# Chunked attention and a gated feed-forward: the second product of the last two blocks in seven products, and another order at the beginning

## The chip, the cores and the metric

One Trainium2 chip, one core. The metric is the device time of one execution in microseconds (us), the median of the runs shown; lower is better. Five engines work side by side: TensorE (PE), VectorE (DVE), ScalarE (ACT), GpSimd (POOL), and SyncE (SP), which issues nearly all DMAs from one queue, in order.

## The reference

q, k and v are 8 x 8 heads x 576 positions x 64, in float32. Attention is within chunks of 64 positions: scores of a chunk are scaled by 1/8, go through a softmax, and weigh v of the same chunk. The result is laid out as x, 4608 tokens x 512. Then

```
h = x @ w_in                              # 512 x 2048, float64 weights
g = h * (1.0 / (1.0 + np.exp(-1.702 * h)))
out = (g @ w_out).astype(np.float32)      # 2048 x 512
```

## The kernel before, in words

**Precision.** Each float32 operand of the feed-forward is split into a high part in TensorE's float32r format and a low part (the rest), and a product is three matmuls: high x high, high x low, low x high, summed in PSUM. The weights arrive as 8-byte words and are converted on the chip by `plan_w`, one column block j of 128 of the 2048 at a time (1 MB of w_in and w_out together): ACT scales (`scale`, L287, `low`, L291), DVE shifts and joins (`shift`, L296, `join`, L300), ACT takes the high part (L305), DVE the low part (L310).

**Blocks.** Tokens go in 36 tiles of 128; four tiles are a block of 512, nine blocks in all. In the first three blocks ("plain", `plan_ffn`) each j has a first product (`h_pe`, L1134 to L1136, 12 matmuls of 512 columns; for the first two j in two halves of 256 columns, `h_half`, L1145 to L1147), the gating on ACT (L1155), its split by ACT and DVE (`g_hi`, L1156, and `g_lo`, L1161), and a second product (`o_pe`, L1171 to L1173, per tile 3 matmuls of 512 columns that add up in the tile's PSUM bank over 16 j).

**Seven products.** The last six blocks go in three pairs (s = 0, 1, 2). Their first product is made by `plan_two` in the scheme of Strassen and Winograd: operands are cut into 2 x 2 quarters, and 7 products of quarters replace 8. A pair has 8 steps p of two column blocks each, every step 7 products (L701 to L703, 6 matmuls of 512 columns), drained by ACT and DVE (`drain`, L714 and L686). The combinations of w_in are made once by `plan_prep` on POOL, ACT and DVE, written to the DRAM tensor `seven`, and read back in pieces of 256 KB into six buffers. The combinations of x (`plan_x`) stay in the slots of w_in that are then free. The second product of these blocks is the plain one: 16 j x 4 tiles x 3 matmuls of 512 columns for each block, from g split by `high` (L744) and `low` (L748).

**Attention.** Tiles 0 to 3 go one by one (`plan_first`): q, k and v rows come by `load_rows` (L359), one DMA for a tile's q and one for its k, 256 KB in packets of 256 bytes (64 floats of one head and position); PE transposes them (L398), ACT and DVE copy them, scores (L419), softmax on DVE, ACT and POOL, transposes of the weights (L447), and x (L463). Later tiles go in pairs (`plan_pair`), whose transposes are made by DVE from the third pair on (L898 and L963).

**Order.** Nothing is ordered by hand in the code: every step is given to `Plan` with its engine, a cost, a rank, the events that it needs, and the buffers that it takes and gives. `Plan.emit` plays the steps through, at each moment starting on each free engine the ready step of least rank, and writes the instructions in that order. Three things overrule the ranks: `ORDER`, which lists the first steps of every engine, `NUDGE`, which adds to the rank of some 70 steps, and `FILL`, three groups of unused matmuls of the identity (`keep_warm`, L1244) among the first steps of PE. One rank unit is one j of a plain block.

## Time and profile before

| | us |
|---|---|
| median of three runs | 829.34 (827.34 to 829.91) |
| span of the profiled execution, first to last instruction | 826.6 |
| PE busy in the span | 814.7 |
| DVE busy | 526.5 |
| ACT busy | 371.2 |
| POOL busy | 94.7 |

Of the profiled execution only its span is given; the three runs are timed without a profile, the lowest of them 0.7 us above that span. Busy time is the union of an engine's instructions. A PE matmul is recorded for longer than the distance to the next one, so PE's rate is read from the starts of neighbouring matmuls.

### The profile page before, as it was taken

How to read it: one execution, taken by the hardware profiler on the slowest of the kernel's cores; microseconds unless marked ns; L12 is line 12 of the kernel's file. 1: busy time of each engine (PE TensorE's matmuls, PEld its weight loads, DVE VectorE, ACT ScalarE, POOL GpSimd, SP SyncE). 2: the span in 40 equal slices, each digit the busy share in tenths (PEclk: the TensorE clock that was granted, in tenths of full speed). 3: DMA queues.
4: the chain of work that ended last, by engine and by line, in shares of the span. 5: the costliest groups of instructions: out<-in, count | busy, mean ns of one | idle time of the engine just before them, and what ended most of it. 6: DMA issues, size and time to landing. Idle time of an engine off the chain costs nothing.

```text
span 826.6 us, 14741 instructions
## 1 busy us (share of the span) xinstructions
PE 814.7 (99%) x5750; PEld 674.1 (82%) x5750; DVE 526.5 (64%) x717; ACT 371.2 (45%) x545; POOL 94.7 (11%) x82
## 2 busy tenths in 40 slices
PE   8899999999999999999999999999999999999998
PEld 7788787888888888888888788888888888888886
DVE  5778977366477789673588686843978543443422
ACT  5889824234346545433446253422653332223322
POOL 1001070000065660000000000000001000000000
PEclk9999999999999999999999999999999999999999
DMA  9998755342386567755574337664441054444101
GB/s 241 323 284 253 235 149 122 56 89 39 68 231 184 121 163 206 189 140 141 145 175 130 50 73 194 169 166 128 128 130 38 26 153 127 119 114 125 52 1 51
DMA packets 233637, 114.24 MB, mean 138 GB/s; under 512 B 185952, under 2 KB 208480, under 8 KB 233568
## 3 DMA queue, kind: packets, MB, share of 16 engines
q1 hardware_dynamic: 233568, 113.30, 52.7%
q8 instruction: 45, 0.74, 0.4%
q14 instruction: 24, 0.20, 0.1%
HBM read 89.13 MB, written 24.12 MB: 137 GB/s over the span
## 4 chain that ended last, share of the span: by engine, by line
PE 87%; DVE 4%; SPq 2%; DMA 2%; ACT 2%; issue 1%; DVEq 0%; ACTq 0%
PE po L1171 15%; PE po L1173 14%; PE po L1172 14%; PE hp L703 9%; PE hp L702 9%; PE hp L701 9%; PE hp L1134 4%; PE hp L1136 4%; PE hp L1135 4%; PE s L914 2%; PE x L988 2%; SPq L359 1%; DMA first_b<-in_v_dram 1%; SPq L855 1%; DMA seven<-w 1%
## 5 line engine op out<-in xcount | busy, mean ns | idle before, releaser
L1171 PE MATMUL po<-w,g_l 128*128 128x512 f32 x576 | 226.5, 393 | 1.1 <-DVE g_l L1161 0.7
L1173 PE MATMUL po<-w,g_h 128*128 128x512 f32 x576 | 224.3, 389 | 0.0
L1172 PE MATMUL po<-w,g_h 128*128 128x512 f32 x576 | 224.3, 389 | 0.0
L1171 PEld LDWEIGHTS po<-w,g_l 128*128 128x128 f32 x576 | 108.1, 188 | 24.6 <-DVE g_l L1161 0.8
L1173 PEld LDWEIGHTS po<-w,g_h 128*128 128x128 f32 x576 | 108.1, 188 | 22.7
L1172 PEld LDWEIGHTS po<-w,g_h 128*128 128x128 f32 x576 | 108.2, 188 | 21.8
L739 ACT ACTIVATE g<-g 128x512 f32<-128x512 f32 x48 | 30.3, 632 | 133.6 <-DVE g L686 133.6
L963 DVE STREAM_TRANSPOSE eT<-e 32x512 f32<-32x512 f32 x120 | 84.2, 702 | 5.1 <-POOL e L944 3.3
L701 PE MATMUL hp<-w,w 128*128 128x512 f32 x224 | 87.1, 389 | 0.0
L702 PE MATMUL hp<-w,w 128*128 128x512 f32 x224 | 87.1, 389 | 0.0
L703 PE MATMUL hp<-w,w 128*128 128x512 f32 x224 | 87.1, 389 | 0.0
L944 POOL TENSOR_TENSOR e<-e,r 128x1024 f32<-128x1024 f32 x16 | 31.6, 1973 | 457.5 <-DVE r L941 255.3
L1134 PE MATMUL hp<-x_l,w 128*128 128x512 f32 x184 | 72.2, 392 | 0.7 <-DVE g_l L1161 0.5
L1136 PE MATMUL hp<-x_h,w 128*128 128x512 f32 x184 | 71.8, 390 | 0.4 <-DVE w L310 0.4
L1135 PE MATMUL hp<-x_h,w 128*128 128x512 f32 x184 | 71.6, 389 | 0.0
L748 DVE TENSOR_TENSOR g_l<-g,g_h 128x512 fp32r<-128x512 f32 x48 | 34.8, 724 | 48.6 <-ACT g_h L744 48.5
L744 ACT ACTIVATE g_h<-g 128x512 fp32r<-128x512 f32 x48 | 30.3, 631 | 75.6 <-PE po L1173 75.3
L898 DVE STREAM_TRANSPOSE qkT<-raw 128x1024 f32<-128x1024 f32 x30 | 37.2, 1242 | 32.9 <-DMA raw<-in_k_dram 19.1
L1161 DVE TENSOR_TENSOR g_l<-hp,g_h 128x512 fp32r<-128x512 f32 (+1 forms) x50 | 33.1, 662 | 35.8 <-ACT g_h L1156 35.4
L686 DVE TENSOR_TENSOR d<-hp,d 128x512 f32<-128x512 f32 x48 | 33.0, 687 | 31.0 <-PE hp L703 30.8
L1155 ACT ACTIVATE hp<-hp 128x512 f32<-128x512 f32 (+1 forms) x50 | 28.4, 569 | 47.8 <-PE hp L1136 43.4
L702 PEld LDWEIGHTS hp<-w,w 128*128 128x128 f32 x224 | 42.1, 188 | 8.7
(117 smaller groups left out, 1206.1 us busy)
## 6 DMA issues: line engine op xcount, KB each, us to landing
w<-seven SPq DMA_DIRECT2D x112, 256.0 KB, 2.9
pieces<-seven SPq DMA_DIRECT2D x56, 256.0 KB, 2.8
seven<-w SPq DMA_DIRECT2D x24, 512.0 KB, 3.8
raw<-in_moe_w_in_dram SPq DMA_DIRECT2D x16, 512.0 KB, 7.7
raw<-in_moe_w_out_dram SPq DMA_DIRECT2D x16, 512.0 KB, 7.1
out_dram<-ob SPq DMA_DIRECT2D x31, 256.0 KB, 3.0
raw<-in_q_dram SPq DMA_DIRECT2D x208, 32.0 KB, 2.1
raw<-in_k_dram SPq DMA_DIRECT2D x208, 32.0 KB, 2.1
```

The source lines that it names most:

```text
L701: nc.tensor.matmul(hp, w[:, 0, c], xl[:, c], start=c == 0, stop=False)
L702: nc.tensor.matmul(hp, w[:, 0, c], xh[:, c], start=False, stop=False)
L703: nc.tensor.matmul(hp, w[:, 1, c], xh[:, c], start=False, stop=c == 1)
L748: nc.vector.tensor_tensor(gl, words(h, late), gh.bitcast(F32), op=ALU.subtract)
L898: nc.vector.transpose(st["tr"][:, i].rearrange("p n (t j) -> p (n t) j", j=32), st["raw"][:, i].rearrange("p n t j -> p (n t) j"),)
L963: nc.vector.transpose(st["et"][po : po + 32, :, 32 * a : 32 * a + 32], st["e"][pi : pi + 32, :, 32 * b : 32 * b + 32],)
L1134: nc.tensor.matmul(hp, wh, xl, start=cc == 0, stop=False)
L1135: nc.tensor.matmul(hp, wh, xh, start=False, stop=False)
L1136: nc.tensor.matmul(hp, wl, xh, start=False, stop=cc == NCC - 1)
L1171: nc.tensor.matmul(po, gl[:, c], w[:, 0, :], start=first, stop=False)
L1172: nc.tensor.matmul(po, gh[:, c], w[:, 0, :], start=False, stop=False)
L1173: nc.tensor.matmul(po, gh[:, c], w[:, 1, :], start=False, stop=last)
```

## The change

It has five parts.

1. **The second product of blocks 7 and 8** (pair s = 2) is made by `plan_o` in seven products of quarters: P4, P1, P5, P7, P3, P6, P2, each over the 8 steps p. A step of a product is 4 tiles x 3 matmuls of 256 columns. Its left operand is a quarter of g of one step p (or a sum of quarters, made in place on DVE: S1 to S4), split by ACT and DVE (`hi` and `lo`) into one of 16 pairs of buffers. Sums of PSUM banks and copies at the end of products (`rd_a1`, `rd_c1`, `c45`, `rd_cX`, `C21`, `C12`, `C22`) give three quarters of the output, P2 with `ends` the fourth, one tile after another.
2. **Combinations of w_out** for four of the seven (`plan_four`): for each p, two sums, four differences and four splits, on DVE and ACT, after the transposes of the weights in attention pairs 22 to 32; they use the attention's buffer `e` and the output's `ob`, go to a DRAM tensor `four`, and come back in 32 pieces of 256 KB.
3. **Pair s = 2 of `plan_two`** runs its 56 products without second products between them (`LASTSTEP`), with two more PSUM banks, and leaves all of g in quarters.
4. **Another beginning.** q and k of two tiles come in one DMA each, 512 KB in packets of 512 bytes (two positions); the transposes become 16 matmuls of 64 x 64 with the identity in place of 4 of 128 x 128. For j = 0 and 1 w_in and w_out are loaded and converted apart (`HALVES`).
5. **The order**: `ORDER`, `NUDGE` and `FILL` go; a table `AT` gives some 250 steps a rank of their own. By it the first DMAs are q and k of tiles 0 and 1, w_in of j = 0, q and k of tiles 2 and 3, v of tiles 1 and 2, w_out of j = 0, w_out of j = 1, both of j = 7, w_in of j = 1, v of tiles 3 and 0, then j = 3 and j = 2.

Cut to its core:

```diff
--- before.py
+++ after.py
...
+AT = {
+    "ld0_0_0": -499.23, "q_0": -296.77, "k_0": -295.51, "raw_0_0": -285.26, "tkp_1": -126.62, "m_0": -86.9,
+    "et_0": -82.39, "wsc_2": -82.01, "raw_0_1": -50.23, "pouts0_7": -45.8057, "raw_1_1": -44.052, "raw_7":
+    -39.292, "raw_1_0": -32.312, "v_3": -32.302, "pouts1_7": -29.0457, "v_0": -26.272, "raw_3": -23.042,
+    "raw_2": -18.532, "qk_0_2_8": -7.5, "wshift_2": -5.028, "xh_3": -3.524, "wj_14": -3.15, "wshift_9": -2.126,
+    "h0_10": -1.7, "gl_10": -1.5, "o_8_0": 0.5, "raw_4": 2.954, "qk_0_1_8": 3.5, "qk_0_3_8": 3.98, "raw_11":
+    4.166, "raw_5": 4.704, "pout0_1": 5, "raw_13": 5.01, "P4_0_5": 5.24, "pout0_6": 7.24, "raw_9": 7.436,
+    "o_1_3": 7.73, "mx_4": 7.836, "w_12": 9.76, "m_4": 9.906, "wshift_15": 10.79, "w_7": 10.902, "o_2_0": 14.43,
...
+}
...
-        rank += self.nudge.get(make, 0.0)
+        rank = self.at.get(make, rank)
...
-    FILL = (5, 2, 5)
+    FILL = ()
...
+    LASTSTEP, OSTEP = 1.75, 2.11
+    RING, AHEAD, AHEAD_S = 16, 2.0, 2.2
+    OSTART = START[-1] + LASTSTEP * NF / 2 + 0.1
+    FOUR = (22, 22, 24, 26, 28, 30, 30, 32)
+    LAST = [n for n in range(NB - 2, NB)]
...
+    HALVES = (0, 1)
...
+        parts = ((0, 1), (1, 1)) if j in HALVES else ((0, 2),)
...
+            def load():
+                w_raw[key] = const.tile([P, width], I64, tag=tag, name=f"raw_{name}")
+                if m == 0:
+                    nc.sync.dma_start(
+                        w_raw[key][:, :512].rearrange("p (cc f) -> p cc f", cc=NCC),
+                        w_in[:, j * P : (j + 1) * P].rearrange("(cc p) f -> p cc f", p=P),
+                    )
+                if m + n == 2:
+                    nc.sync.dma_start(w_raw[key][:, width - 512 :], w_out[j * P : (j + 1) * P, :])
...
         def load(i):
+            if ("first", u) not in held:
+                a = const.tile([P, 2048], F32, tag=slot(0), name=f"first_a_{u}")
+                held["first", u] = a.rearrange("p (i h e d) -> p i h e d", i=2, h=H, e=2)
+            for b, s, o, c in spans(u * P, 2 * P):
+                nc.sync.dma_start(
+                    held["first", u][o // 2 : (o + c) // 2, i].rearrange("p h e d -> p h (e d)"),
+                    (q, k)[i][b, :, s : s + c, :].rearrange("h (j e) d -> j h (e d)", e=2),
+                )
...
+            rows = slice(64 * t2, 64 * t2 + 64)
             for n in range(NP):
-                nc.tensor.transpose(
-                    st["ps", i][:, n], st["raw"][:, i, 2 * n : 2 * n + 2, :].rearrange("p h d -> p (h d)"), ident
-                )
+                for e in range(2):
+                    for h in range(2):
+                        nc.tensor.matmul(
+                            st["ps", i][64 * h : 64 * h + 64, n].rearrange("p (t e) -> p t e", e=2)[:, :, e],
+                            held["first", u - t2][rows, i, 2 * n + h, e],
+                            ident[rows, rows],
+                            start=True,
+                            stop=True,
+                        )
...
-        plan.add(DMA, (1, 1.2, 1024), u - 103, lambda: load(0), make=ev("q"), take=[slot(0)])
-        plan.add(DMA, (1, 1.2, 1024), u - 102.9, lambda: load(1), make=ev("k"))
+        if t2 == 0:
+            plan.add(DMA, (1, 1.5, 1024), u - 103, lambda: load(1), make=ev("k"), take=[slot(0), f"w{NF - 3 - 2 * u}"])
+            plan.add(DMA, (1, 1.5, 1024), u - 102.9, lambda: load(0), need=[ev("k")] * 0, make=ev("q"))
+            plan.add(None, 0, u - 95, None, need=[ev("s"), f"s_{u + 1}"], give=[slot(0), f"w{NF - 3 - 2 * u}"])
...
+        def bank(i):
+            q = 7 * p + i
+            return f"po{2 + q // 2 % 2}" if last and q % 2 else "hp"
...
+    T_ORDER = ("T1", "T3", "T4", "T2")
...
+    def plan_four(p):
...
+        def whole(u):
+            if u == 0:
+                st["a"] = const.tile([P, 2, 2, 256], F32, tag="e", name=f"four_a_{p}")
+            w = wt[2 * p + u][:, 1].bitcast(F32)
+            nc.vector.tensor_tensor(
+                st["a"][:, u].rearrange("p k f -> p (k f)"), w[:, 0], w[:, 1], op=ALU.add
+            )
+
+        def sums():
+            (b11, b12), (b21, b22) = [[st["a"][:, u, k] for k in range(2)] for u in range(2)]
+            tt = nc.vector.tensor_tensor
+            tt(b11, b12, b11, op=ALU.subtract)
+            tt(b12, b22, b12, op=ALU.subtract)
+            tt(b22, b22, b11, op=ALU.subtract)
+            tt(b21, b21, b22, op=ALU.subtract)
...
+        u = FOUR[p]
+        rank = RANKS[(u - TB) // 2] - 5
+        e = lambda a: f"{a}_{p}"
+        plan.add(DVE, 0.69, rank, lambda: whole(0), need=[f"et_{u}"] + ([f"tlo3_{p - 1}"] if p else []), make=e("ta0"), take=["e"], port=True)
+        plan.add(DVE, 0.69, rank, lambda: whole(1), need=[e("ta0")], make=e("ta"), port=True)
+        plan.add(DVE, 1.7, rank, sums, need=[e("ta")], make=e("tsum"), port=True)
+        for i in range(4):
+            plan.add(ACT, 0.36, rank, lambda i=i: hi(i), need=[e("tsum")] + [e(f"tlo{i - 1}")] * (i > 0), make=e(f"thi{i}"), take=["ob"])
+            plan.add(
+                DVE, 0.41, rank, lambda i=i: lo(i), port=True, need=[e(f"thi{i}")], make=e(f"tlo{i}"), give=["e"] * (i == 3),
+            )
+            plan.bulk(0.8, rank, lambda i=i: out4(i), need=[e(f"tlo{i}")], make=e(f"tout{i}"), give=["ob"], after=4.0)
+        plan.add(None, 0, rank, None, need=[e(f"tout{i}") for i in range(4)], make=e("tout"))
...
+    def plan_o():
...
+        PRODUCTS = (
+            ("P4", "Y", True, (1, 1), "T4"),
+            ("P1", "X", True, (0, 0), (0, 0)),
+            ("P5", "Z", True, (1, 1), "T1"),
+            ("P7", "Y", False, (0, 1), "T3"),
+            ("P3", "Z", False, (0, 1), (1, 1)),
+            ("P6", "X", False, (1, 1), "T2"),
+            ("P2", "W", True, (1, 0), (1, 0)),
+        )
...
+            open_, stop = fresh and (t % 2 == 0 or a == "W"), p == H - 1
+            nc.tensor.matmul(o, gh[:, c], w[:, 0], start=open_ and p == 0, stop=False, skip_group_check=not open_)
+            nc.tensor.matmul(o, gh[:, c], w[:, 1], start=False, stop=False, skip_group_check=not open_)
+            nc.tensor.matmul(o, gl[:, c], w[:, 0], start=False, stop=stop, skip_group_check=not open_)
...
+        def w_add(what, by, p, fn, need):
+            plan.add(DVE, 0.69, rank(number[by], p) - AHEAD_S, fn, port=True, need=need, make=f"{what}_o_{p}")
+
+        for p in range(H):
+            w_add("S1", "P5", p, lambda p=p: sum_((1, 1), (0, 1), (1, 1), ADD)(p), [f"cl_{number['P4']}_{p}", ge(p, 0, 1)])
+            w_add("S3", "P7", p, lambda p=p: sum_((0, 1), (0, 0), (0, 1), SUB)(p), [f"S1_o_{p}", ge(p, 0, 0)])
+            w_add("S2", "P3", p, lambda p=p: sum_((1, 1), (1, 1), (0, 0), SUB)(p), [f"cl_{number['P5']}_{p}", f"S3_o_{p}"])
+            w_add("S4", "P3", p, lambda p=p: sum_((0, 1), (1, 0), (1, 1), SUB)(p), [f"S2_o_{p}", f"cl_{number['P7']}_{p}", ge(p, 1, 0)])
...
+                take = (["g"] if r < 2 else []) if n < RING else [f"cb{r}"]
+                need = [source[name](p)] + ([freed[r - 2]] if 2 <= n < RING else [])
+                if n:
+                    need.append(f"ch_{(n - 1) // H}_{(n - 1) % H}")
+                plan.add(ACT, 0.6, rank(q, p) - AHEAD, lambda q=q, p=p, r=r: hi(q, p, r), need=need, make=f"ch_{q}_{p}", take=take)
+                plan.add(DVE, 0.69, rank(q, p) - AHEAD, lambda q=q, p=p: lo(q, p), port=True, need=[f"ch_{q}_{p}"], make=f"cl_{q}_{p}")
...
+                plan.add(
+                    PE, 1.44, rank(q, p), lambda q=q, p=p, kk=kk: [mm(q, p, t, kk) for t in range(TB)], need=need + [before],
+                    make=f"O{q}_{p}", take=take, give=give,
+                )
...
+        for t in range(TB):
+            for p in range(H):
+                plan.add(
+                    PE, 0.36, rank(END, 2 * t + p / 4), lambda p=p, t=t: mm(END, p, t, None), need=[f"cl_{END}_{p}", before],
+                    make=f"O{END}_{p}_{t}", take=[BANKS["W"][t]] if p == 0 else [],
+                )
...
+        for i in range(2):
+            both = lambda n, i=i: f"{n}_{i}"
+            plan.add(ACT, 0.6, after("P4"), lambda i=i: copy("Y", i, "a1"), need=[done("P4")], make=both("rd_a1"), take=["tmp"] * (1 - i))
+            plan.add(ACT, 0.6, after("P1"), lambda i=i: copy("X", i, "c1"), need=[done("P1")], make=both("rd_c1"), take=["ob", "ob"] * (1 - i))
+            plan.add(DVE, 0.69, after("P5"), lambda i=i: with_("Z", i, "a1", "a1", SUB), need=[done("P5"), both("rd_a1")], make=both("c45"))
+            plan.add(ACT, 0.6, after("P6"), lambda i=i: copy("X", i, "c12"), need=[done("P6")], make=both("rd_cX"), take=["tmp"] * (1 - i))
+            plan.add(DVE, 0.69, after("P6"), lambda i=i: with_("Y", i, "c21", "c12", ADD), need=[both("rd_cX"), done("P7")], make=both("C21"), take=["tmp"] * (1 - i), give=[BANKS["Y"][i]])
+            plan.add(DVE, 0.69, after("P6"), lambda i=i: with_("Z", i, "c12", "c12", ADD), need=[both("C21"), done("P3")], make=both("C12"))
+            plan.add(DVE, 0.69, after("P6"), lambda i=i: c22(i), port=True, need=[both("C12"), both("c45")], make=both("C22"))
...
+        for t in range(TB):
+            plan.add(DVE, 0.43, after("P6"), lambda t=t: ends(t), need=[f"O{END}_{H - 1}_{t}", "rd_c1_1"], make=f"C11_{t}")
+            plan.add(
+                DMA, (len(list(spans((n0 * TB + t) * P, P))), 0.5), rank(END, 2), lambda t=t: store("c1", 0, 0, t), need=[f"C11_{t}"],
+                make=f"st_C11_{t}",
+            )
...
+        if n in LAST:
+            if n == LAST[0] and j % 2 == 0:
+                plan_two(TWOS - 1, j // 2)
+            return
...
+    for p in range(NF // 2):
+        plan_four(p)
+    plan_o()
```

## Rows read from the trace of the kernel before

**Rows 1.** The profile's page: its head and the busy time, share of the span and instructions of each engine.
```profile
span 826.6 us, 14741 instructions
...
PE 814.7 (99%) x5750; PEld 674.1 (82%) x5750; DVE 526.5 (64%) x717; ACT 371.2 (45%) x545; POOL 94.7 (11%) x82
```

**Rows 2.** The view of windows: stretch in us, its length, then PE, PEld, DVE, ACT and POOL, each with busy time in us and number of instructions; the granted TensorE clock; the DMA engines' busy share; GB/s. Here the stretch after the start and before the end.
```profile
100.00:820.00 720.00, 719.02 (x4880) 594.19 (x4879) 449.26 (x621) 286.32 (x437) 87.61 (x71) 1.00 0.47 120
```

**Rows 3.** The view of waits of PE alone, in us, times, longest.
```profile
PE x L463 <- DMA first_b<-in_v_dram: 1.8, 1, 1.8
PE x L463 <- DVE x_l L474: 1.4, 1, 1.4
...
PE hp L1134 <- DVE g_l L1161: 0.5, 1, 0.5
PE hp L1136 <- DVE w L310: 0.4, 1, 0.4
```

**Rows 4.** The timeline of PE in the last microseconds: start in us, us, engine, line, operation, out<-in. Two third products of neighbouring steps of a second product, the second of them the last matmul of the kernel.
```profile
821.77 0.39 PE L1173 MATMUL po<-w,g_h 128*128 128x512 f32 x1
...
822.45 0.39 PE L1173 MATMUL po<-w,g_h 128*128 128x512 f32 x1
```

**Rows 5.** The same view where the two-half first products stand, 24 of them in a row, each with its own weight load: the first and the last.
```profile
31.54 0.28 PE L1145 MATMUL hp<-x_l,w 128*128 128x256 f32 x1
...
34.30 0.28 PE L1147 MATMUL hp<-x_h,w 128*128 128x256 f32 x1
```

**Rows 6.** The view of lines, shapes kept apart: line, engine, operation, out<-in, shape, count | busy us, mean ns of one | idle before. The evictions and conversions that the added work is priced with.
```profile
L748 DVE TENSOR_TENSOR g_l<-g,g_h 128x512 fp32r<-128x512 f32 x48 | 34.8, 724 | 48.6 <-ACT g_h L744 48.5
...
L686 DVE TENSOR_TENSOR d<-hp,d 128x512 f32<-128x512 f32 x48 | 33.0, 687 | 31.0 <-PE hp L703 30.8
...
L744 ACT ACTIVATE g_h<-g 128x512 fp32r<-128x512 f32 x48 | 30.3, 631 | 75.6 <-PE po L1173 75.3
...
L1161 DVE TENSOR_TENSOR g_l<-hp,g_h 128x256 fp32r<-128x256 f32 x4 | 1.7, 419 | 1.4 <-ACT g_h L1156 1.4
L1156 ACT ACTIVATE g_h<-hp 128x256 fp32r<-128x256 f32 x4 | 1.5, 385 | 0.1
```

**Rows 7.** Windows of the last 180 us, in which the old order still mixes first and second products.
```profile
640.00:820.00 180.00, 180.00 (x796) 149.05 (x795) 71.43 (x107) 52.27 (x86) 0.00 (x0) 1.00 0.29 82
```

**Rows 8.** DMA issues of the page: out<-in, engine, count, KB each, median us from issue to landing.
```profile
w<-seven SPq DMA_DIRECT2D x112, 256.0 KB, 2.9
```

**Rows 9.** Windows of the stretch in which the change puts eight preparations, and of its three fullest parts.
```profile
300.00:560.00 260.00, 259.59 (x1837) 214.96 (x1828) 187.43 (x263) 112.18 (x169) 19.02 (x12) 1.00 0.59 148
300.00:320.00 20.00, 20.00 (x191) 16.77 (x182) 18.52 (x22) 14.35 (x23) 9.49 (x7) 1.00 0.67 187
440.00:460.00 20.00, 19.59 (x87) 15.90 (x86) 18.46 (x25) 12.69 (x19) 1.91 (x1) 1.00 0.50 125
480.00:500.00 20.00, 20.00 (x90) 16.56 (x89) 18.33 (x28) 10.40 (x15) 1.91 (x1) 1.00 0.42 97
```

**Rows 10.** Windows of the start; the DMA share and GB/s stand at the end of each row.
```profile
0.00:4.00 4.00, 2.64 (x12) 2.64 (x13) 0.00 (x0) 1.28 (x1) 0.70 (x6) 1.00 0.54 121
4.00:8.00 4.00, 3.63 (x42) 3.04 (x42) 0.66 (x1) 1.20 (x2) 0.00 (x0) 1.00 1.32 218
...
12.00:16.00 4.00, 3.26 (x70) 2.71 (x70) 3.83 (x10) 3.01 (x7) 1.17 (x2) 1.00 1.13 330
16.00:20.00 4.00, 3.70 (x64) 3.25 (x60) 3.68 (x7) 3.62 (x6) 1.96 (x2) 1.00 1.15 322
```

**Rows 11.** The chain of waits at the start: start us, us, what. The DMA of it is the load of the value rows of tile 0, from its issue to its landing.
```profile
13.11 8.21 DMA first_b<-in_v_dram
21.46 0.73 PE x L463 x32
22.21 0.61 ACT x_h L471
22.84 0.70 DVE x_l L474
```

**Rows 12.** The timeline of PE from the first dense products on: the first half of the first product, x of tile 3, the first second product, and the first whole first product (for the third column block of weights).
```profile
27.03 0.36 PE L1145 MATMUL hp<-x_l,w 128*128 128x256 f32 x1
...
28.63 0.69 PE L463 MATMUL x<-first_b 64*64 64x64 f32 x32
30.03 0.50 PE L1171 MATMUL po<-w,g_l 128*128 128x512 f32 x1 [0.71 <-DVE g_l L1161]
...
39.49 0.39 PE L1134 MATMUL hp<-x_l,w 128*128 128x512 f32 x1
```

**Rows 13.** Windows of ACT's and DVE's load while the weights are converted.
```profile
28.00:90.00 62.00, 60.76 (x443) 50.35 (x443) 49.04 (x57) 56.40 (x70) 2.19 (x1) 1.00 0.89 256
90.00:100.00 10.00, 10.00 (x103) 8.10 (x104) 9.86 (x11) 9.26 (x11) 0.00 (x0) 1.00 0.98 320
```

**Rows 14.** The chain of waits in that stretch.
```profile
88.03 1.13 DVE w L310
89.17 0.61 DVE g_l L1161
...
89.83 0.50 PE hp L1134
```

**Rows 15.** The timeline at the very end: the last copy out of PSUM.
```profile
822.87 0.69 DVE L1185 COPY ob<-po 128x512 f32<-128x512 f32 x1 [0.67 <-PE po L1173]
```

364 lines of the change are left out of this document (258 added, 106 removed), and 49 rows, old and new, of tables (AT, NUDGE, ORDER).

## The prediction

> **What bounds the kernel now.** I read the page first, then the windows after the start, PE's waits, and last the start, where PE has holes. PE is busy 814.7 of 826.6 us [rows 1], but that is recorded time, longer than the spacing of matmuls, so the windows matter more: from 100 to 820 us PE stands still for 0.98 us in all, at full clock [rows 2]. Waits that ended at PE in the whole run are a few of 0.4 to 1.8 us, the longest in the attention of the first tiles [rows 3]. So behind the start the time is the sum of the matmul spacings. There are two places to gain, fewer spacings and an earlier start, and in the middle the change can only lose.
>
> The spacing: like matmuls of neighbouring steps start at 821.77 and 822.45 with three spacings between, 0.227 us each at 512 columns [rows 4]. At 256 columns, each with a load of weights of its own, 24 in a row start from 31.54 to 34.30, 23 spacings: 0.120 us [rows 5]. Half the columns cost 53% of the spacing.
>
> **Second product of blocks 7 and 8.** Removed: 2 blocks x 16 j x 4 tiles x 3 = 384 matmuls at 0.2267 us, 87.0 us. Added: 7 products x 8 steps x 4 tiles x 3 = 672 at 0.120 us, 80.6 us. PE gains **6.4 us**, all on the path. Seven eighths alone would have given 10.9; the rest goes into the shorter matmuls. The Trainium skill, "TensorE: Matmul & The Clock Gate", section "Back-to-back issue gap", gives an isolated spacing of N/2.4 + 2.5 ns: 109 ns for 256 columns; it says too that with weight loads both operations set the spacing, so that the formula counts too little at small N. By 109 ns the gain would be 13.6 us. The row has 120 ns in just this pairing of loads and products, and I take the row.
>
> What feeds these products: 56 splits on ACT (0.631 us) and DVE (0.724 us), 32 sums on DVE (0.69 us), 8 sums over two tiles at the ends of products, 4 of one tile [rows 6]. DVE: 56 x 0.724 + 32 x 0.69 + 8 x 0.69 + 4 x 0.42 = 69.8 us beside 80.6 of PE; ACT: 56 x 0.631 plus six copies, 39 us. Over the whole part DVE has 10 us to spare, but S1 to S4 come early: up to the first step of P3, 46 us in, it must do 33 splits, between 27 and 32 sums and two evictions, 43.9 to 47.4 us. Splits that begin ahead (16 buffer pairs) give some lead. Old DVE load there was 71 of 180 us [rows 7]. Bounds 0 and 3 us lost; I take **+0.8**.
>
> The 56 first products of pair 2 in a row take 42 x 0.2267 = 9.5 us for a step; DVE drains are 7 x 0.69 = 4.8 us of that, ACT 5 x 0.63 = 3.2 us: no cost. A piece is needed every 1.36 us; issue to landing is 2.9 us [rows 8], against six buffers, so 8.2 us; if that cover were gone, one piece late costs its lateness once for each turn of six. The 32 pieces of `four` come slower than that: no cost. The steps at the start of `plan_o` need only quarters that are ready several us before: P4 of step 7 needs the gate after the fifth of the last seven first products, and ten us of other steps stand before it.
>
> The tail: the last copy out starts at 822.87 and takes 0.69 us [rows 15], and the span ends 3.0 us after that. It becomes a sum over 256 columns (0.42 us by the 128 x 256 row of [rows 6]) and a store half as big: **-0.3**. Twelve of the 16 stores are issued before it, during P2; if they weren't, SP's queue would put some 0.5 us each before the last.
>
> **Combinations of w_out.** On DVE a step is 2 x 0.69 + 8 x 0.42 = 4.7 us, eight steps 37.9 us; on ACT 8 x 4 x 0.385 = 12.3 us [rows 6]. They fall between 300 and 560 us, where DVE works 187 of 260 and ACT 112 [rows 9]: there is room for 72.6 us in all, but in the bursts of attention 1.5 to 1.7 us of 20 are left. What waits behind them on DVE are the drains of first products, whose PSUM buffers PE takes next, and the next attention pair, which waits for `e`. On SP 32 writes and 32 reads of 256 KB are added; a write that waits for its split holds piece loads, which have 8.2 us, and q/k rows of later pairs. POOL has nothing new. One cost with the new ranks of all the rest, which reorder a stretch that lost 0.98 us and so can't give more than that: bounds -1 and +5, I take **+0.7**, near the low end, since the same kind of burst today costs PE only 0.4 us in 20 [rows 9].
>
> **The beginning.** Up to 20 us the DMA engines are saturated: q and k in 256-byte packets run at 218 GB/s, and the mix of weights and v behind them at 322 to 330 GB/s [rows 10]. With v at the 218 of the same packets, weights come out at about 370 (an estimate: 2.6 MB in 8 us, of which about 0.5 MB is v). The last thing that the first product waits for is v of tile 0, landing at 13.11 + 8.21 = 21.3 us, then x, its high and its low part, to 23.5 [rows 11]. PE's order then puts x, transposes and unused matmuls first, and the first product starts at 27.03; behind it x of tile 3 (0.69 us) and a wait of 0.71 us stand in its way again [rows 12].
>
> After: before v of tile 0 (again last) stand 2.1 MB of q and k, 3.15 MB of weights (j = 7 among them, which nobody wants yet), with 1.05 MB of v: 8.5 us + 4.8 us + q and k. For 512-byte packets there is no row; between 218 and 370 GB/s they take 9.6 to 5.7 us, I take 300, halfway, 7.0 us. 0.48 MB has moved by 4.0 us [rows 10], so transfers begin at 1.8; v lands at 22.1 us (20.8 to 24.7), the first product can start 2.1 us later, at 24.2 (22.9 to 26.8), with all four x behind it: 27.03 - 24.2 + 0.7 + 0.7 = 4.2 us earlier (1.6 to 5.5). The Trainium skill, "DMA: Bandwidth & Descriptors", section "Specifications", has 512 bytes as the least transfer for line rate; by that q and k would go at the weights' 370 GB/s and v would land at the early end. The transposes (16 of 64 x 64 where x does 32 in 0.73 us [rows 11], so 0.4 us or twice that) lie beside transfers: no cost. Loading w_in of j = 0 early moves ACT's conversion to where it idles.
>
> That gain must pass the weights' conversion. From 28 to 90 us ACT works 56.4 of 62 us, then DVE 9.86 of 10 [rows 13], and at 89.8 us PE waits on DVE, which had done the weights' low part and then the split that frees the buffer [rows 14]. If DVE and ACT are not earlier there, an earlier start ends in that wait. ACT has 5.6 us of slack before it and starts earlier, but gets shorter instructions for j = 0 and 1. I let half of it through: **-2.2**, bounds 0 and -5.5.
>
> **Sum**: -6.4 + 0.8 - 0.3 + 0.7 - 2.2 = -7.4 us, on the profiled span of 826.6: 819.2. The median, 829.34, lies 2.7 us (0.3%) above that span, the lowest run 0.7; I put the same difference on the median: **821.9**. A difference of 0.3%, 2.5 us, is about what a measurement of this kernel can tell from none.
>
> **Rivals.**
> *The beginning gives nothing*: the old start comes back at the wait at 89.8 us, the rest as in the sum: -5.2, 824.1. For it speaks [rows 14], against it ACT's 5.6 us. Chance 0.12.
> *DVE becomes the bound in `plan_o`*: besides no gain at the start, S1 to S4 come late by the full 3 us: -6.4 + 3 - 0.3 + 0.7 = -3.0, 826.3. Chance 0.14, parted by the bound of 2.5 us: 0.06 faster, 0.08 the same.
> *The other side, combinations of w_out starve PE*: drains queue behind them in the bursts, PE's two first-product buffers stay full, and PE waits. Its place is 300 to 560 us; from 8.1 + 2.5 = 10.6 us of uncovered DVE time, 28% of the 37.9, the kernel is slower (8.1 is the sum without its +0.7). With half uncovered, 19 us: +10.9, 840. Against: 72.6 us of room, and PE can do second products meanwhile; for: the bursts at 18.3 to 18.5 of 20. Chance 0.14, 0.12 of it slower, 0.02 the same.
> *Half the columns at half the spacing*: 672 x 0.1133 = 76.2 us, if the 24 in a row were slow for being at the start: 4.5 us less than the sum, 817.4 (the formula of "Back-to-back issue gap" in the Trainium skill's "TensorE: Matmul & The Clock Gate" would give 814.7). Against it 23 even spacings of 120 ns. Chance 0.05.
> The change does what it says in products and packets, as the code of the new loads shows; I give that no rival.
>
> **The numbers.** The sum as it stands has 0.55; its own range is 817.5 to 825.5. Faster 0.55 + 0.12 + 0.06 + 0.05 = 0.78, the same 0.08 + 0.02 = 0.10, slower 0.12. The range, 816.5 to 829, leaves out the slow rival and the far ends of the bounds.
>
> **What would show it.** 672 matmuls of 256 columns spaced 0.120 us in the last 80 us; no PE wait over 1 us there, and if there is one, on a DVE split in P7 or P3. First dense product at 23 to 27 us with v of tile 0 landing two us before; then whether PE waits for weights between 60 and 100 us. From 300 to 560 us DVE at about 225 of 260 us with PE idle for at most some us. The forecast is wrong if PE idles over 3 us there, if the new spacing is not 0.120, or if first products start after 27 us.

## The result and the profile after

| | before | after |
|---|---|---|
| median, us | 829.40 (827.34 to 829.91, 5 runs) | 832.56 (830.06 to 836.86, 5 runs) |
| span of the profiled execution | 826.6 | 830.8 |
| v of tile 0 landed | 21.3 | 24.7 |
| first dense product | 27.03 | 32.43 |
| last matmul starts | 822.45 | 827.32 |

The ratio is 1.0051, 95% interval 1.0026 to 1.0076: slower by half a per cent, where 821.9 was forecast. The profiled execution is the one at the median.

The page's head and busy time, against [rows 1]:

```profile
span 830.8 us, 16156 instructions
...
PE 813.8 (98%) x6238; PEld 688.0 (83%) x6238; DVE 590.3 (71%) x867; ACT 394.6 (47%) x609; POOL 91.5 (11%) x82
```

DVE has 64 us more to do; PE's recorded time says little, as before. The windows (columns as in [rows 2]), against [rows 9] and [rows 7], show that the added work does no harm where it stands:

```profile
300.00:560.00 260.00, 260.00 (x1854) 214.33 (x1853) 208.24 (x323) 119.50 (x192) 20.12 (x14) 1.00 0.64 168
740.00:820.00 80.00, 80.00 (x641) 78.82 (x640) 59.35 (x96) 35.62 (x63) 0.00 (x0) 1.00 0.37 115
```

PE is never idle in either, although DVE went from 187 to 208 us of 260. The combinations themselves run from 372 to 618 us, later than the 300 to 560 of the forecast; from 300 to 820 us PE is idle for 0.13 us in all. PE's timeline inside a new product, and DVE's at the end:

```profile
784.72 0.28 PE L1033 MATMUL acc_Y<-pieces,w 128*128 128x256 f32 x1
...
785.92 0.28 PE L1034 MATMUL acc_Y<-pieces,w 128*128 128x256 f32 x1
```

```profile
827.64 0.42 DVE L1048 TENSOR_TENSOR c<-acc_W,c 128x256 f32<-128x256 f32 x1 [2.45 <-PE acc_W L1034]
```

Ten spacings in 1.20 us: 0.120 each, as in [rows 5]. So the loss lies elsewhere. PE's waits, against [rows 3]:

```profile
PE hp L1478 <- DVE g_l L1505: 4.1, 3, 2.5
PE eTp L523 <- POOL first_b L518: 2.8, 1, 2.8
PE qkTp L470 <- issue: 2.1, 1, 2.1
...
PE s L495 <- issue: 1.0, 1, 1.0
```

Of these only the first is not at the start. Two of them have no releaser ("issue"): PE's data was there and it issued nothing. The chain of waits from the start, in order of time:

```profile
0.73 4.24 DMA first_a<-in_q_dram
5.01 4.08 PE qkTp L470 x124
9.09 1.95 PE s L495 x61
11.11 0.46 PE qkTp L470 x15
11.57 2.07 issue
13.64 4.02 PE qkTp L470 x103
17.98 0.85 PE s L495 x13
18.83 1.00 issue
19.84 2.82 PE s L495 x48
22.66 0.69 PE eTp L523 x4
...
25.09 0.70 DVE z L512
...
28.61 0.93 DVE wtmp L343
...
30.71 0.61 DVE x_l L550
...
31.37 1.13 PE x L539 x32
32.50 0.51 PE hp L1489
```

In [rows 11] the chain was a transfer, v of tile 0. Here it is PE itself up to 22.7 us, with the small transposes (L470) and scores (L495) of four tiles, and then 8.7 us of what stands behind the last scores: their softmax on ACT, DVE and POOL, x and its parts, with shifts and joins of weights (`wtmp`) between them in DVE's order. v is not in it, though it landed at 24.7.

**PE's debt.** The rest of the text compares kernels by one sum: the start of a matmul less the spacings of all dense matmuls ahead of it (0.227 us at 512 columns, 0.120 at 256; small ones at 17 ns, those of 128 columns at 109). It is what PE has lost by then, by its start, waits or half clock; the last column is the work itself, up to the last matmul. Columns are by work done; 90 us of work is at about 125 us, 260 at about 300.

| work done, us | 0 | 50 | 90 | 250 | 300 | 400 | 500 | end | all work |
|---|---|---|---|---|---|---|---|---|---|
| before | 27.0 | 28.7 | 30.0 | 31.4 | 31.8 | 31.8 | 32.6 | 32.6 | 789.9 |
| after | 32.4 | 34.9 | 36.8 | 38.2 | 42.8 | 43.0 | 43.5 | 43.9 | 783.5 |
| products_only | 27.4 | 30.0 | 31.8 | 36.3 | 36.7 | 39.1 | 52.8 | 62.9 | 783.5 |
| begin_only | 31.8 | 34.0 | 41.4 | 42.2 | 46.0 | 47.2 | 50.3 | 59.3 | 789.9 |
| old_begin | 27.6 | 37.0 | 37.4 | 38.1 | 39.8 | 41.3 | 42.2 | 43.1 | 783.5 |
| half_tp | 28.1 | 30.5 | 35.4 | 36.6 | 41.4 | 42.1 | 42.7 | 43.0 | 783.5 |
| rev40 | 32.6 | 35.0 | 39.4 | 40.3 | 53.2 | 53.3 | 54.1 | 54.1 | 789.9 |
| hybrid40 | 27.5 | 29.9 | 31.8 | 35.6 | 40.0 | 41.5 | 42.3 | 42.6 | 783.5 |
| hybrid_seam | 27.1 | 29.3 | 29.4 | 30.9 | 32.9 | 34.7 | 36.7 | 37.0 | 783.5 |

The work fell by 6.4 us. The debt rose by 11.3: 5.4 at the first product, 1.4 more by 125 us, 4.2 between 290 and 300 us, and only 0.3 behind that. The net, 4.9, less 0.7 gained in the tail, is the span's 4.2.

The 4.2 is one wait and the half clock behind it. DVE's timeline there:

```profile
284.40 1.23 DVE L1275 TENSOR_TENSOR e<-s,m 128x1024 f32<-128x1024 f32 x1
290.37 2.37 DVE L1242 STREAM_TRANSPOSE qkT<-raw 128x1024 f32<-128x1024 f32 x2 [4.74 <-DMA raw<-in_q_dram]
292.66 1.18 DVE L1282 TENSOR_REDUCE z<-e 128x16 f32<-128x1024 f32 x1
...
294.25 0.63 DVE L1505 TENSOR_TENSOR g_l<-hp,g_h 128x512 fp32r<-128x512 f32 x1
294.80 2.74 DVE L634 TENSOR_TENSOR w<-g,w 128x512 fp32r<-128x512 f32 x2
```

DVE stood 4.74 us for the last rows of q of a pair, which SP had issued at 286.24, behind sixteen issues of k that took it 8.81 us; `g_l`, whose input had been ready for over 3 us, was queued behind, and PE waited 2.5 us for it (at 294.9), with half clock from 295.9 to 299.3.

### The profile page after: what moved, and what is told of

It is laid out like the page before. It is cut to its first block, busy times and chain, and to the rows that moved or that the text cites. A ratio compares the mean times of both kernels' runs of the same rounds, so it can differ in the third digit from the quotient of the medians.

```text
span 830.8 us, 16156 instructions
## 1 busy us (share of the span) xinstructions
PE 813.8 (98%) x6238; PEld 688.0 (83%) x6238; DVE 590.3 (71%) x867; ACT 394.6 (47%) x609; POOL 91.5 (11%) x82
## 4 chain that ended last, share of the span: by engine, by line
PE 89%; SPq 3%; DVE 3%; DMA 3%; issue 1%; ACT 1%; DVEq 0%; ACTq 0%
PE po L1515 12%; PE po L1516 11%; PE po L1517 11%; PE hp L785 9%; PE hp L786 9%; PE hp L787 9%; PE hp L1478 4%; PE hp L1480 4%; PE hp L1479 4%; SPq L1199 3%; PE s L1258 2%; PE x L1332 1%; DMA seven<-w 1%; PE qkTp L470 1%; PE acc_Y L1034 1%
## 5 line engine op out<-in xcount | busy, mean ns | idle before, releaser
L1515 PE MATMUL po<-w,g_l 128*128 128x512 f32 x448 | 176.9, 395 | 0.1
L1516 PE MATMUL po<-w,g_h 128*128 128x512 f32 x448 | 175.0, 391 | 0.0
L1517 PE MATMUL po<-w,g_h 128*128 128x512 f32 x448 | 174.9, 390 | 0.0
L1515 PEld LDWEIGHTS po<-w,g_l 128*128 128x128 f32 x448 | 84.5, 189 | 18.7 <-DVE g_l L836 0.3
L1517 PEld LDWEIGHTS po<-w,g_h 128*128 128x128 f32 x448 | 84.4, 188 | 17.8
L1516 PEld LDWEIGHTS po<-w,g_h 128*128 128x128 f32 x448 | 84.4, 188 | 16.9
L1288 POOL TENSOR_TENSOR e<-e,r 128x1024 f32<-128x1024 f32 x16 | 31.3, 1955 | 457.2 <-DVE r L1285 335.1
L1505 DVE TENSOR_TENSOR g_l<-hp,g_h 128x512 fp32r<-128x512 f32 (+1 forms) x50 | 33.2, 663 | 47.4 <-ACT g_h L1500 47.0
L1242 DVE STREAM_TRANSPOSE qkT<-raw 128x1024 f32<-128x1024 f32 x30 | 36.6, 1233 | 21.4 <-PE s L1258 8.8
L785 PEld LDWEIGHTS hp<-w,w 128*128 128x128 f32 x224 | 42.0, 188 | 9.7 <-DVE f L766 0.6
L787 PEld LDWEIGHTS hp<-w,w 128*128 128x128 f32 x224 | 42.1, 188 | 8.8
L786 PEld LDWEIGHTS hp<-w,w 128*128 128x128 f32 x224 | 42.1, 188 | 8.6
L1478 PEld LDWEIGHTS hp<-x_l,w 128*128 128x128 f32 x184 | 34.5, 188 | 13.0 <-DVE g_l L1505 5.9
```

Source lines behind the costliest of these rows:

```text
L785: nc.tensor.matmul(hp, w[:, 0, c], xl[:, c], start=c == 0, stop=False)
L786: nc.tensor.matmul(hp, w[:, 0, c], xh[:, c], start=False, stop=False)
L787: nc.tensor.matmul(hp, w[:, 1, c], xh[:, c], start=False, stop=c == 1)
L1242: nc.vector.transpose(st["tr"][:, i].rearrange("p n (t j) -> p (n t) j", j=32), st["raw"][:, i].rearrange("p n t j -> p (n t) j"),)
L1478: nc.tensor.matmul(hp, wh, xl, start=cc == 0, stop=False)
L1505: nc.vector.tensor_tensor(gl[:, c], hp, gh[:, c].bitcast(F32), op=ALU.subtract)
```

## The experiments

A profiled execution is one draw: runs of one kernel lie within some 3 to 8 us of each other. hybrid40 and hybrid_seam below have one order up to 290 us, and their debts there are 35.6 and 31.1. So the debt of a single profile is read to about 5 us, a smaller difference only where rows show the wait behind it, and times by medians.

### Each part alone

**products_only** is the kernel before with the new second product and its combinations, under the old ranks; **begin_only** the changed kernel with the old second products; **old_begin** the changed kernel with the old beginning.

```diff
 products_only            # rest from the kernel after
+ORDER, NUDGE, FILL, plan_first of the kernel before;  HALVES = ()
-    plan.at.update(AT)
 begin_only
+LAST = [];  last = False              # no plan_four, no plan_o
 old_begin                # as products_only, but
+        rank = self.at.get(make, rank)     # new ranks where ORDER lists nothing
```

> The kernel before with the second product in seven products and its preparations, but with the old beginning and the old order lists (ranks of the other steps as before). Theory A (the products keep their gain, the new beginning and the new ranks lose more): 829.4 - 6.4 - 0.3 = 822.7, within 821.5 to 824.5; first dense product at 27.0 us, 672 matmuls spaced 0.120 us at the end, no PE wait over 1 us between 300 and 560 us. Rival B (preparations and held buffers cost in the middle what the products save, the beginning is harmless): 829 to 832, with PE waits of 5 us or more in the middle.

> The changed kernel with the old second product for the last two blocks, so the new beginning and the new ranks alone. Theory A: 829.4 + 6.6 (start) + 4.4 (the stall near 292 us and the slow clock behind it) = 840, within 836 to 842; first dense product near 32.4 us, PE stopping at 11.6 and 18.8 us with no releaser. Rival B: 825 to 829, the start worth what was forecast.

> The changed kernel with the old beginning (loads, transposes, weights in one piece, order lists and unused matmuls for the first steps), and the new table of ranks for all other steps. Theory A: if the stall near 292 us comes with the new table, 822.7 + 4.4 = 827; if it comes from the late start, 822.7. Rival B: 829 to 832.

Measured: products_only 849.74 us (846.77 to 851.81), ratio 1.0224 [1.0199, 1.0249]; begin_only 855.13 (853.48 to 856.99), 1.0302 [1.0279, 1.0324]; old_begin 834.23 (831.51 to 839.8), 1.0057 [1.0034, 1.0080]. None of the three lies in a range of its expectation, neither the theories' nor the rivals'. Each part alone, products_only and begin_only, is far worse than both together. The windows of products_only show where:

```profile
440.00:480.00 40.00, 32.08 (x245) 24.87 (x243) 31.24 (x46) 17.36 (x28) 2.15 (x1) 0.91 0.47 121
620.00:700.00 80.00, 73.20 (x491) 57.88 (x490) 52.09 (x81) 30.23 (x50) 2.16 (x1) 1.00 0.28 82
```

PE loses 12 us in the first, 8 of them idle and the rest at half clock, with DVE at 31 of 40; the changed kernel has PE at 40.00 there with DVE at 34. So the added work can starve PE, as the rival on the slow side said, but not by its amount: by the order. Under the new ranks of the changed kernel it costs next to nothing. begin_only has those ranks without the work that they were made for, and loses 12 us behind 400. old_begin has the old start and the new ranks, and loses 9.4 us in its first 50 us of work, among them one wait of 3.2 us for a `g_l` on DVE. What follows: a part is not priced by leaving out the other, unless the order is fitted too; the later runs therefore splice orders.

### The beginning

**many_warm** delays PE of the kernel before and touches nothing else: 112 unused matmuls of 64 x 64 at the start in place of 7 of 128 x 128.

```diff
-            nc.tensor.matmul(warm, ident, ident, start=True, stop=True)          # x7
+            nc.tensor.matmul(warm[r, :64], ident[r, r], ident[r, r], ...)        # x112, halves in turn
```

> The kernel before; the 7 unused matmuls of 128 x 128 at the very start are 112 of 64 x 64 instead, which take about as long (112 x 2 at 17 to 34 ns is 3.8 to 7.6 us against 3.4) but give PE 210 records of products and as many of loads more to read before 12 us. They compute nothing that is used. Theory C (PE ran out of instructions, whose fetch stands behind the saturated DMA engines): PE stops once for 1 to 2.5 us with no releaser before 20 us, first dense product at 28 to 30 us, 830.5 to 832. Rival D (the two stops were waits on data that the trace does not name): no such stop; if the small matmuls end by 7 us, the start moves by what they are longer, otherwise 829.4.

Measured: 832.08 us (830.59 to 836.31, 10 runs), ratio 1.0027 [1.0011, 1.0044]. The first dense product came at 31.08, 4.05 later, the end of the profiled execution 2.4 later; by the ratio the median is 2.2 later. More than half of this late start is paid. The stop of theory C did not come: PE ran through all 224 records, 42 ns apart, until 10.8 us.

**half_tp** takes both tiles of a pair through one transpose, with 64 matmuls for 128, and moves one score behind a copy. **fewer_warm** has 3 unused matmuls at the start for 7.

```diff
 half_tp
-    held["first", u - t2][rows, i, 2 * n + h, e], ident[rows, rows]              # 64 x 64, 4 n
+    held["first", u - t2][:, i, 4 * t2 + 2 * n + h, e], ident                    # 128 x 64 by 128, 2 n
 fewer_warm
-    WARM = 7
+    WARM = 3
```

> The changed kernel with the transposes of the first four tiles for both tiles of a pair at once: 64 matmuls whose weights are 128 rows of 64 and whose moving operand is the whole identity (128 columns), in place of 128 with 64 rows and 64 columns; copies out as many and as large as before, order of the steps the same but for one score behind a copy. Theory (the beginning is lost on PE: 1.02 us for each of eight groups of small matmuls, and two stops of 2.07 and 1.00 us for instructions): a group takes 0.5 to 0.7 us, the first stop stays at about the 449th PE record, which is then a later operation, first dense product at 28.5 to 30.5 in place of 32.4, time 829 to 831. Rival (transfers or DVE and ACT set the start; PE's groups lie beside them): groups get shorter, the first dense product stays at 31.5 to 32.5, time 832 to 833. Second rival (a matmul of 128 columns takes twice as long): groups stay at 1.0 us, no change.

> The changed kernel with 3 unused matmuls at the start instead of 7 (8 PE records fewer, the order the same). Theory (the stops of PE without releaser at 11.57 and 18.83 us are a wait for instructions, so they stand at a fixed count of records): the first stop again before record 449 counted from PE's first, eight records further in the program; its length 1.5 to 2.5 us. Rival (the stop is of that operation or its data): it stays ahead of the same transpose, which is then record 441. Time within 1 us of 832.6.

half_tp: the first dense product came at 28.09, 4.3 earlier than in the changed kernel, earlier than the theory said; the time did not follow, 834.58 us (831.70 to 837.07), ratio 1.0062 [1.0043, 1.0080]. Its chain at the start:

```profile
15.05 9.28 DMA first_b<-in_v_dram
...
24.46 1.17 PE x L555 x32
25.65 0.61 ACT x_h L563
26.28 0.70 DVE x_l L566
27.03 1.13 PE x L555 x32
28.16 0.51 PE hp L1505
```

The transfer of v bounds the start again, as forecast for the change, but barely: PE's first x waited 0.43 us for it.

```profile
24.46 1.13 PE L555 MATMUL x<-first_b 64*64 64x64 f32 x32 [0.43 <-DMA first_b<-in_v_dram]
```

So in the changed kernel PE's small work, with the softmax behind it, had taken v's place, at a cost of 4.3 us. The groups didn't get much shorter (its four of a pair 3.54 us, against 3.86): what went are both stops. In this the second rival was right: a record of 128 columns takes 56 ns, one of 64 takes 30. But of these 4.3 us the debt keeps only 1.4 at 125 us, after waits for DVE at 85.2 and 118.3, and 0.9 at the end; the medians, by their ratios, are alike. The time gained nothing. Even this start is 1.1 us later than that of the kernel before: v landed at 24.3, where it had landed at 21.3.

fewer_warm, one run at 835.13: a first stop near record 449 was not seen (PE came to it later), so the expectation failed in its letter. The next one was seen, in PE's timeline:

```profile
17.96 0.90 PE L495 MATMUL s<-first_tr 64*64 64x64 f32 x23
20.70 0.80 PE L495 MATMUL s<-first_tr 64*64 64x64 f32 x10 [1.84 <-issue]
```

In the changed kernel the stops come after 222 and 350 of PE's matmul records: 128 matmuls and as many weight loads apart, 256 together. Here one comes again after record 350, behind 23 scores instead of 13. It stays with the count, not with the operation.

The traces also show what PE waited for. The DMA view of the changed kernel's first 40 us has a queue for instructions:

```profile
q8 instruction: 4, 0.07, 0.7%
```

Its packets in the trace are transfers of 16 KB. In the changed kernel two of them end at 12.22 and 18.42 us, and PE goes on at 13.64 and 19.84; in fewer_warm one ends at 19.27, and PE goes on at 20.70. after_moved, begin_only, rev40 and mid4 have the same beginning, and they stop after records 222 and 350 or after 350 alone. In all nine stops of these six traces PE goes on 1.2 to 1.4 us after such a transfer has ended. In many_warm the transfer had ended at 9.33, and PE came to record 222 only at 10.4: no stop. The trace doesn't say whose instructions a transfer brings, but count and times agree in every stop: PE waits for instructions. The Trainium skill, "Runtime: NRT & Kernel Launch", section "Instruction fetch mechanics", has blocks of 256 instructions that are fetched ahead, with a cost that is mostly hidden: the 256 agree with the trace, the hiding doesn't, with stops of 2.07, 1.00 and 1.84 us where PE ran through small matmuls of 30 ns.

### Single waits, by moving single steps

**after_moved** lifts the `g_l` that waits behind the transposes at 290 us ahead of them; **old_moved** does so in old_begin, and for one more gate; **mid4** gives the steps of rank 4 to 40 their old ranks.

```diff
+MOVES = (("gh_42", "behind", "ex_18"), ("gl_42", "behind", "gh_42"))                  # after_moved
+    ... ("gh_6", "before", "ex_4"), ("gl_6", "before", "wj_13")                       # old_moved besides
 mid4
+        rank = rank + self.nudge.get(make, 0.0) if 4 <= rank < 40 else self.at.get(make, rank)
```

> The changed kernel with one pair of steps put elsewhere in the order: the high and low part of the gate of first product 42 (ACT g_h, DVE g_l) stand ahead of the two transposes of the raw q and k of pair 20 on DVE, instead of behind them and behind the sum of an exponential. Everything else as in the changed kernel (832.56). Theory (in order: DVE stood 4.74 us for the last rows of q, with g_l, whose inputs were ready at 290.9, queued behind it): the PE wait of 2.54 us at 294.93 and the 3.4 us of half clock behind it go, nothing of 1 us takes their place, 4.4 us less: 828.2 (827 to 829.5). Rival (DVE and ACT have too much to do there since the combinations were added): the wait comes back within 30 us at the scores or the transposes that are now later, gain under 1.5 us: 831 to 832.6.

> The kernel with the new products and combinations and the old beginning (834.23) with four steps put elsewhere: the gate of first product 6 on ACT ahead of the exponential of tile 4 and its low part on DVE ahead of the last of three joins of weights; the gate of first product 42 ahead of the transposes of pair 20 as in the other kernel of this call. Theory (single waits by order, each with the half clock behind it): the waits of 3.37 us at 77.0 and 1.21 us at 293.4 go, with the 3.4 us of half clock behind the first: 6.3 us less, 828 (826.5 to 829.5). Rival (ACT and DVE are full between 60 and 90 us, the wait moves to the next gate): 832 to 834.

> The changed kernel with the old ranks for the steps of rank 4 to 40 alone (some 50 to 290 us); beginning and the rest as in the changed kernel. Theory (the new ranks of that stretch cost 4 us, the wait at 294 us among them, and the beginning the other 5 to 6): 827 to 829. Rival (any order of that stretch loses as much once the start is 5 us later and its waits fall elsewhere): 831 to 836, with waits of 2 us and more in it at other places.

All three failed, and their rivals' ranges with them. after_moved 836.08 us (832.47 to 839.62), ratio 1.0083 [1.0059, 1.0108]; old_moved 836.48, 1.0089 [1.0068, 1.0109]; mid4 860.73, 1.0381 [1.0353, 1.0410]. DVE in after_moved:

```profile
292.73 0.69 DVE L1516 TENSOR_TENSOR g_l<-hp,g_h 128x512 fp32r<-128x512 f32 x1 [5.31 <-ACT g_h L1511]
...
295.62 1.18 DVE L1293 TENSOR_REDUCE z<-e 128x16 f32<-128x1024 f32 x1
...
297.21 2.93 DVE L645 TENSOR_TENSOR w<-g,w 128x512 fp32r<-128x512 f32 x2
300.06 0.68 DVE L1516 TENSOR_TENSOR g_l<-hp,g_h 128x512 fp32r<-128x512 f32 x1
```

The moved `g_l` was in time, but DVE had idled 5.3 us ahead of it all the same, now for ACT's `g_h` and not for rows of q; the next `g_l` stood behind the backlog, and PE waited 2.5 us at 300.8, much as the rival said. So lifting one step past the idle time only moved the wait; that the idle time itself is the cause, no run shows, since none took it away. In mid4, PE waits 8.6 and 6.6 us ahead of 90 us: old ranks with the new start are the worst of all.

### Splices: the old order up to about 290 us, the new behind it

**hybrid40** has the old beginning and order for ranks under 40, the new products and ranks behind; **rev40** is its mirror with the old second products.

```diff
 hybrid40                 # products_only, and in Plan.add
+        rank = rank + self.nudge.get(make, 0.0) if rank < 40 else self.at.get(make, rank)
 rev40                    # begin_only, and
+        rank = self.at.get(make, rank) if rank < 40 else rank + self.nudge.get(make, 0.0)
```

> The new products and combinations with the old beginning, the old order for every step of rank under 40 (step for step that of the kernel before up to first product 43, about 290 us) and the new ranks from there (from second product 48 on step for step the order of the changed kernel). Theory (products are worth 6 us, the combinations cost nothing under the new ranks, and all of the loss stands ahead of 300 us: the new beginning and the new order of that stretch): what PE had lost by 300 us is that of the kernel before, 32 to 36 us (27 of it the start), 1 to 2 more to the end, so 823 to 826, faster than both. Rival (the combinations cost 5 us or more wherever they stand): PE loses over 5 us behind 300 us, 829 or more.

> The mirror of that: new beginning and new ranks under rank 40, the old order behind it, the old second products without the new combinations. Theory: it has the changed kernel's loss ahead of 300 us and none of its gain: 5 to 11 us over the kernel before, 835 to 841, with what PE has lost by 300 us at 40 to 46 us in place of 32, and under 2 more behind. Rival (the start costs nothing at the end, and the products gave less than 6): 829 to 832.

hybrid40: 829.28 us (826.53 to 831.32, 12 runs), ratio 0.9986 [0.9968, 1.0003]; the profiled run is its slowest. rev40: 848.98, 1.0235 [1.0206, 1.0264]. By its time hybrid40 came out as its rival had it, and PE lost 7.0 us behind 300 us, where the rival had over 5 and the theory 1 to 2. rev40 has 42.6 us of debt after 280 us of work, before its seam (the place where one order hands over to the other), where the changed kernel has 42.8 and the kernel before 31.8. In all traces with both the new beginning and the new ranks the debt there is 41.4 to 46.0, in all with the old of both 31.3 to 36.7. So nearly the whole loss belongs to the beginning and the new order of the first 290 us. Behind that rev40's seam cost 10.6 that nobody had counted. Of hybrid40's 7.0, 4.1 are its seam, in PE's and ACT's rows:

```profile
PE hp L808 <- DVE w L657: 2.3, 1, 2.3
```

```profile
321.38 0.61 ACT L654 ACTIVATE w<-g 128x512 fp32r<-128x512 f32 x1
326.88 0.60 ACT L1550 ACTIVATE ob<-po 128x512 f32<-128x512 f32 x1 [4.88 <-DMA out_dram<-ob]
327.37 0.62 ACT L855 ACTIVATE g_h<-d 128x512 fp32r<-128x512 f32 x1
327.89 0.62 ACT L654 ACTIVATE w<-xs 128x512 fp32r<-128x512 f32 x1
```

ACT stood for an output buffer, with a split (L654) behind it that PE needed. **hybrid_seam** puts the copy behind the splits, **hybrid44** and **hybrid47** put the seam elsewhere.

```diff
+MOVES = (("ob_2_0", "behind", "h6x_0_1"), ("st_2_0", "before", "st_2_2"))            # hybrid_seam
+    ... if rank < 44 else ...     /     ... if rank < 47 else ...                     # hybrid44, hybrid47
```

> As the kernel of old order up to rank 40 and new ranks behind, with one copy of outputs on ACT (of block 2, tile 0), which waited 4.88 us for its buffer, behind the two splits for the first two-block products instead of ahead of them, and its store accordingly. Theory (the seam's wait is that copy in order on ACT): the PE wait of 2.41 us at 329.9 and the half clock behind it go, 3 to 4 us less: 825 to 827. Rival (the wait comes back within 20 us): 828.5 to 830.

> The same with the seam at rank 44 in place of 40. Theory (only the seam costs): 825 to 832 by what the new seam costs, and the time less what PE loses between 300 and 360 us is 825 or less. Rival (the combinations cost): PE loses 3 us or more behind 360 us.

> The same with the seam at rank 47. Theory and rival as for 44: 825 to 832 by the seam; PE's loss behind 360 us under 2.5 us by the theory, 3 or more by the rival.

hybrid_seam: **826.61 us** (825.04 to 828.59, 12 runs), ratio 0.9960 [0.9946, 0.9974], as its theory said, and faster than both kernels: by the ratio 3.3 us under the kernel before, about half of the 7.1 that products and tail are worth. Its longest waits behind the start, in the view of PE's waits:

```profile
PE hp L819 <- DVE w L668: 1.3, 1, 1.3
PE po L1549 <- DVE ob L1563: 1.3, 1, 1.3
PE hp L819 <- DVE d L800: 0.9, 1, 0.9
```

hybrid44 and hybrid47: 856.94 (1.0329 [1.0306, 1.0351]) and 844.46 (1.0187 [1.0161, 1.0212]). Behind 360 us, where 2.5 were allowed to the theory, each lost over 20: in this the rival came true. hybrid_seam loses 4.1 us there too, where the changed kernel loses 1.1 and the kernel before 0.8. So the combinations are nearly free only under the very order of the changed kernel: the new ranks fit with each other and with what stands ahead, and a seam four ranks further starves PE again.

## Why the prediction was wrong

**Right: the products.** -6.4 was forecast, and the work fell from 789.9 to 783.5. The spacing of 0.120 us held, and the rival of half the columns at half the spacing is out. The Trainium skill's isolated gap ("TensorE: Matmul & The Clock Gate", "Back-to-back issue gap"), which would have been 0.109, is not what this pairing of loads and products shows.

**Mis-sized: DVE in the last part.** +0.8 was taken; PE has no idle time from 740 to 820 us, so it is 0. The tail gave 0.7 where 0.3 was forecast.

**The combinations of w_out**, +0.7 with bounds of -1 and +5: behind 300 us the debt of the changed kernel grows by 1.1, in the kernel before by 0.8. But the same sentence took the new ranks for a rearrangement that could cost little in a stretch that had lost 0.98 us. A wait at 294.9 cost 4.2, ahead of the combinations: within the bound, far from the value taken. The six traces with the new beginning and the new ranks lose 2.3 to 5.4 us at that place (250 to 270 us of work), those with the old of both 0.1 to 0.5, and old_begin 1.4. A late start by itself is not the reason, since half_tp, 4.3 us earlier, still loses 4.7 there; but the runs can't part the order's share from that of the new beginning's transfers: mid4 and after_moved, which tried, lost more.

**The step that failed: the beginning, -2.2.** The first product was forecast at 24.2 us and came at 32.43, 5.4 later than before. half_tp parts these 8.2 us into three. First, 2.2: v of tile 0 landed there at 24.3, where 22.1 was taken, still inside 20.8 to 24.7. Second, 1.7: from v to the first product it took 3.8 us, where 2.1 was taken; two groups of x stand in it, each at half clock. Third, 4.3: PE's small work of the changed kernel. The first two alone would have made the start 1.1 us later than before, so the -2.2 had the wrong sign without the third. The packets of q and k were not the error: the DMA engines moved 303 to 331 GB/s between 4 and 8 us, where 300 was taken and 218 stood in [rows 10]; from 8 to 12 us, with v's 256-byte packets in the mix, it was 280. The windows:

```profile
4.00:6.00 2.00, 1.70 (x26) 1.41 (x26) 0.00 (x0) 0.00 (x0) 0.00 (x0) 1.00 1.19 303
6.00:8.00 2.00, 2.00 (x80) 1.93 (x76) 0.00 (x0) 1.19 (x2) 0.00 (x0) 1.00 1.12 331
8.00:12.00 4.00, 3.57 (x124) 3.42 (x121) 2.69 (x5) 2.36 (x4) 0.00 (x0) 1.00 1.22 280
```

What failed most is the sentence that costed the transposes at nothing because they lie beside transfers. It priced a group at 0.4 us or twice that, by 32 of x in 0.73 us; but the 32 there are records, two for each float32 matmul, so the row itself gave 0.73 for 16. Measured is 1.02 (128 records, four groups, in 4.08 us), for eight groups in a row, on the one engine that had the transposes, the scores and the first products to do in order. With them came two stops for instructions, 3.07 us, and half clock (1.2 GHz) from 16.0 to 22.8 and from 29.6 to 36.5, each some us after PE had stood idle (11.6 to 13.6, 24.7 to 27.5); the kernel before has 3.4 us of it at the start, half_tp 10.2. The stops alone are not all of it: in rev40, mid4 and fewer_warm PE stops only once, but the first transposes are 48 ns apart instead of 30, and the first product comes at 32.6 to 33.2 as well.

The cover was named, and not held against PE's own time, nor against what stands behind it: from the end of the last scores (22.66) to the first product it is 9.8 us of softmax, x and its parts. Summed from 5.0 us on, 8 x 0.8 for the transposes, four scores of 0.93 and these 9.8 give about 25 us, close to the 24.2 by way of v; the trace of before shows no stop that would have tipped it. The bound of 0 for the beginning, "gives nothing", should have been a loss.

**Not passed on.** The forecast let half of an early start through, because of [rows 14]. half_tp fits that in the profile: of 4.3 us earlier, 1.4 remain at 125 us and 0.9 at the end. many_warm's late start is passed on by 2.4 of 4.05. These are single draws, and no run shows that a fixed order treats an early start otherwise than a late one.

**The rivals.** The slow side's mechanism, combinations that starve PE on DVE, was not what made the change slower; it did appear in products_only, hybrid44 and hybrid47, by order and not by amount. The sign came from rivals that were not on the list: the beginning itself losing, and the new order losing ahead of 300 us, before any combination.

**What stays open** is how much of the 5.6 us of debt that the changed kernel takes on, beyond the kernel before, between the first product and 300 us would go under ranks fitted to the new start. hybrid_seam shows only that it goes with the old start and the old order together; with the old start and the new ranks (old_begin) it doesn't. Open too is how much of the start is DVE's order, with its joins of weights ahead of x's low part: no run moved them.

## What to carry to other kernels

When a step is taken as hidden beside transfers, add up what the engine that does it must do in order until the transfers end, add what other engines must do behind that, count its instructions as well as their time, and let the bound go to a loss. An order fitted to one timing is part of the kernel's cost: price a rearrangement by what it does to the steps behind a late one, and test parts by splicing orders, since leaving a part out under the other's ranks told of the ranks (849.7 and 855.1) and not of the part. The gain was there, in PE's work, and came out at the end only where the start and the order ahead of it were left alone, and there by half.

## What the runs showed of the hardware

- PE stops for instructions: nine stops of 0.4 to 2.6 us in the six traces with a start of 64 x 64 matmuls, each after 222 or 350 matmul records, each over 1.2 to 1.4 us after a 16 KB transfer of the instruction queue had ended. many_warm ran 224 records of 42 ns at its start without such a stop; its transfer had ended 1.1 us before PE came to that count.
- In fewer_warm, mid4 and rev40 the first 125 small transposes were spaced 48 ns, against 28 to 30 ns in the changed kernel, after_moved and begin_only. In the first three the profile's clock records begin only at 12.9 to 13.7 us, in the others at 4.7 to 5.8; ahead of the first record a window prints 1.00 without having read it. The number of unused matmuls is not the reason: mid4 and rev40 have all seven.
- With the granted clock read as 1.00 from 4.8 us on, 64 records of 128 moving columns and 128 rows of weights (32 matmuls, half_tp) took 3.54 us, and 128 of 64 by 64 (64 matmuls, begin_only and after_moved) 3.57: these small float32 matmuls cost by their columns, and halving their number saved instructions but no time.
